# One head group of three V loads on eight of the sixteen DMA engines, 32 KB per read

## The chip, the cores and the metric

The kernel runs on one core of a Trainium2 chip. The metric is the time of one execution on the device in microseconds, read from repeated runs. The experiments ran on several chips, each of them beside runs of the kernel before on the same chip.

## The reference

It is one attention step with a cache: 32 batches, 4 new tokens each, 32 query heads in 4 groups, 2048 cached keys of 128 numbers, all bfloat16.

```python
B, Sq, D = 32, 4, 1024
Hq, Hkv, Sk, Dh = 32, 4, 2048, 128
q = (x @ wq).reshape(B, Sq, Hq, Dh).transpose(0, 2, 1, 3)
scores = einsum("bhqd,bhkd->bhqk", q, repeat(k_cache)) * (Dh ** -0.5)
o = einsum("bhqk,bhkd->bhqd", softmax(scores), repeat(v_cache))
return o.transpose(0, 2, 1, 3).reshape(B, Sq, Hq * Dh) @ wo
```

Keys and values are 2 MB each per batch, 134 MB in all. Nearly all of the kernel's 151 MB of reading is that.

## The kernel before

Each batch is one K load and one V load of 2 MB. K has three buffers in SBUF (the memory on the chip, 128 partitions) and so has V. PE, the matrix engine, transposes K, multiplies with the queries, transposes the probabilities and multiplies with V; ScalarE (ACT in the profile) and VectorE (DVE) move PE's results from PSUM to SBUF and do the softmax. SP issues the loads. The parts that matter here:

```python
def load_k(b):                       # partition = (group, r): 16 KB in one piece per partition
    p.dma("sp", lambda e: e.dma_start(
        K_sb[:, b % NKB, :, :], k_cache[b].rearrange("g (r t) d -> (g r) t d", r=R)),
        [("fill", b - NKB, NFILL - 1)] if b >= NKB else [], ("k", b), f"s_k{b % NKB}")

def load_v(b):                       # 128 partitions x 4 groups x 4 KB
    src = v_cache[b].rearrange("g (p t) d -> p g (t d)", p=128)
    dst = V_sb[:, b % NVB, :, :, :].rearrange("p g t d -> p g (t d)")
    waits = [("pv", b - NVB)] if b >= NVB else []
    if b < B - 1:
        p.dma("sp", lambda e: e.dma_start(dst, src), waits, ("v", b), f"s_v{b % NVB}")
    else:
        ...                          # the last V load: one copy per group

for b in range(NKB):
    load_k(b)
for b in range(B):
    if b + NKB < B:
        load_k(b + NKB)
    load_v(b)
    ...                              # loads 2 to 5 also bring a quarter of wo

def pe_pv(i):
    ...
    waits = waits + [("pt", i, 0), ("pt", i, 1), ("v", i)]
```

In the trace the completion semaphore of a load takes 16 steps. They are read here as one for each of the page's 16 DMA engines that ends its share. The kernel makes PE wait for all 16.

Of the kernel before, what the change touches and what calls it, by code (L numbers as in the profile page):

```python
# [6 lines left out]
ALU = mybir.AluOpType  # L7
AX = mybir.AxisListType
BF16 = mybir.dt.bfloat16
F32 = mybir.dt.float32  # L10


class _Program:
# [43 lines left out]
def bass_standalone__gqa_block_cached__sampling_kernel(  # L57
# [8 lines left out]
    B, Sq, D = x.shape  # L66
# [10 lines left out]
    KT = D // 128  # L77
    NKB = 3
    NVB = 3
    NFILL = 8  # L80
    TB = T // NFILL
    NRING = 4
# [9 lines left out]
    with ExitStack() as es:  # L92
        def sbuf(name, shape, dtype):
            return es.enter_context(nc.sbuf_tensor(name, shape, dtype))
# [3 lines left out]
        K_sb = sbuf("K_sb", [128, NKB, T, Dh], BF16)  # L98
        V_sb = sbuf("V_sb", [128, NVB, G, TV, Dh], BF16)
        KT_sb = sbuf("KT_sb", [128, TV, G, R * C], BF16)  # L100
# [8 lines left out]
        ident = sbuf("ident", [128, 128], BF16)  # L109
        mx = sbuf("mx", [128, B], F32)  # L110
        negmx = sbuf("negmx", [128, B], F32)
        ssum = sbuf("ssum", [128, B], F32)
        rinv = sbuf("rinv", [128, B], F32)

        ps_s = es.enter_context(nc.psum_tensor("ps_s", [128, Sk], F32))
        ps_r = es.enter_context(nc.psum_tensor("ps_r", [128, 4, 512], F32))
        ring = [ps_r[:, i, :] for i in range(NRING)]
# [5 lines left out]
        p = _Program()  # L123
# [8 lines left out]
        def load_k(b):  # L132
# [4 lines that stand above are left out]
        def load_v(b):  # L137
            src = v_cache[b].rearrange("g (p t) d -> p g (t d)", p=128)
            dst = V_sb[:, b % NVB, :, :, :].rearrange("p g t d -> p g (t d)")
            waits = [("pv", b - NVB)] if b >= NVB else []  # L140
            if b < B - 1:
                p.dma("sp", lambda e: e.dma_start(dst, src), waits, ("v", b), f"s_v{b % NVB}")
            else:
                for g in range(G):
                    p.dma("sp", lambda e, g=g: e.dma_start(dst[:, g, :], src[:, g, :]), waits, ("v", b, g), f"s_vl{g}")
# [8 lines left out]
# [4 lines that stand above are left out]
            if b in (2, 3, 4, 5):  # L158
                load_wo(b - 2)
# [21 lines left out]
        for j in (4, 5, 6, 7, 0, 1, 2, 3):  # L181
            src = (ps_s if j < 4 else ps_r[:, :, :].rearrange("p a b -> p (a b)"))[:, (j % 4) * 512:(j % 4 + 1) * 512]
            src = src.rearrange("p (hh b s) -> p hh b s", hh=4, b=B, s=Sq)
            dst = QT_sb[:, :, 4 * j:4 * j + 4, :].rearrange("p b hh s -> p hh b s")
# [9 lines left out]
        def slot(free):  # L194
            n = len(freed)
            freed.append(free)
            return ring[n % NRING], [freed[n - NRING]]
# [3 lines left out]
        def pe_fill(b, f):  # L201
            buf, waits = slot(("kt", b, f))
            buf = slot_of["kt", b, f] = buf.bitcast(BF16)
            for q in range(TB):
                c, v = q // (TB // C), q % (TB // C)
                t = c * TV + f * TB // C + v
                p.op("pe", lambda e, q=q, t=t: e.transpose(  # L207
                    buf[:, q * 128:(q + 1) * 128], K_sb[:, b % NKB, t, :], ident[:, :]),
                    waits + [("k", b), "ident"] if q == 0 else [], ("fill", b, f) if q == TB - 1 else None)
# [25 lines left out]
        def pe_qk(i):  # L235
            waits = [("kt", i, f) for f in range(NFILL)]
            waits += [("qe", j) for j in range(Hq // 4)] if i == 0 else [("exp", i - 1)]
            for c in range(4):
                for g in range(G):
                    p.op("pe", lambda e, c=c, g=g: e.matmul(  # L240
                        ps_s[32 * g:32 * (g + 1), c * 512:(c + 1) * 512],
                        lhsT=QT_sb[:, i, REP * g:REP * (g + 1), :],
                        rhs=KT_sb[:, 4 * c:4 * (c + 1), g, :],
                        start=True, stop=True, tile_position=(0, 32 * g)),
                        waits, ("qk", i) if (c, g) == (3, G - 1) else None)

        def pv_mm(buf, i, g, t, waits, done):
            p.op("pe", lambda e: e.matmul(  # L248
                buf[32 * g:32 * (g + 1), 0:Dh],
                lhsT=PT_sb[:, i % 2, t, 32 * g:32 * (g + 1)],  # L250
                rhs=V_sb[:, i % NVB, g, t, :],
                start=(t == 0), stop=(t == TV - 1), tile_position=(0, 32 * g)), waits, done)

        def pe_pv(i):
            buf, waits = slot(("o", i))
            slot_of["o", i] = buf
            waits = waits + [("pt", i, 0), ("pt", i, 1), ("v", i)]
            for t in range(TV):
                for g in range(G):
                    pv_mm(buf, i, g, t, waits if t == 0 and g == 0 else [],  # L260
                          ("pv", i) if (t, g) == (TV - 1, G - 1) else None)
# [54 lines left out]

        for f in range(NFILL):
            pe_fill(0, f)
            evac(0, f)
        L = B - 1  # L320
        for i in range(B):
            pe_qk(i)
            softmax_max(i)
            if i >= 3:
                pe_ot(i - 3)
                ot_evac(i - 3)
                if i > OG and i % OG == 2:
                    oproj(i // OG - 1)
            if i < L:
                for f in (0, 1):  # L330
                    pe_fill(i + 1, f)
                    evac(i + 1, f)
            softmax_exp(i)
            if i < L:
                for f in range(2, NFILL):
                    pe_fill(i + 1, f)
                    evac(i + 1, f)
            softmax_rinv(i)
            if i >= 2:
                pe_pv(i - 2)  # L340
                o_evac(i - 2)
            if i == L:
                p.op("dve", lambda e: e.tensor_scalar(P_sb[:, :], P_sb[:, :], rinv[:, L:L + 1], None, op0=ALU.mult),  # L343
                     [("rinv", L)], ("pn", L))
            for f in range(2):
                pe_pt(i, f, ("pn", L) if i == L else ("exp", i))
                evac_pt(i, f)


        pe_ot(L - 2)  # L350
        ot_evac(L - 2)
        pe_pv(L - 1)
        o_evac(L - 1)
        y_l = ps_s[:, 0:512]
        n = NOG - 1

        def pv_last(g):
            buf, waits = slot(None)
            for t in range(TV):
                p.op("pe", lambda e, t=t: e.matmul(  # L360
                    buf[:, 0:32], lhsT=V_sb[:, L % NVB, g, t, :], rhs=PT_sb[:, L % 2, t, 32 * g:32 * (g + 1)],
                    start=(t == 0), stop=(t == TV - 1)),
# [77 lines left out]
```

## Time and profile before

| | before |
|---|---|
| time, median | 383.13 us (382.86 to 383.46, 3 runs) |
| DMA load queue, share of 16 engines' span | 97.2% |
| PE, DVE, ACT busy | 72%, 72%, 54% |
| last K load (batch 31) lands | 353.36 us |
| DMA packets, typical time | 4 KB 160 ns, 16 KB 615 ns |

The page cuts the span in 40 slices of 9.5 us. The first line below is the granted PE clock in tenths, the second the busy share of the DMA engines in tenths, the third what they moved in GB/s. Page of the kernel before:

```profile
PEclk9999999999788699999999999999999999999978
DMA  8999999999999999999999999999999999999981
GB/s 328 437 426 420 412 422 410 413 391 411 403 409 412 417 418 420 415 407 417 422 416 413 420 419 412 419 416 417 413 416 420 416 414 420 416 419 410 351 315 32
```

The engines are busy throughout, mostly at 400 to 420 GB/s. The queues on the same page (packets, megabytes, share of the 16 engines' span):

```profile
q1 hardware_dynamic: 27104, 151.49, 97.2%
q8 instruction: 46, 0.75, 0.8%
```

Queue 8 is instruction fetch: 46 packets of 16 KB. The chain of waits that ended last (shares of the span, by engine and then by line) is mostly a wait for K:

```profile
DMA 59%; PE 17%; ACT 11%; DVE 9%; issue 3%; SPq 1%
DMA K_sb<-in_k_cache_dram 52%; DMA V_sb<-in_v_cache_dram 7%; ACT KT_sb L219 6%; ACT P_sb L285 5%; DVE KT_sb L217 5%; PE ps_r L207 4%; PE ps_r L296 3%; DVE mx L280 3%; PE ps_r L248 3%; PE ps_r L225 2%; PE ps_s L240 2%; PE ps_s L296 1%; DVE PT_sb L231 1%; PE ps_r L360 0%; SPq L129 0%
```

In order of time (start, length, what) three pieces of this chain show its end:

```profile
331.59 21.78 DMA K_sb<-in_k_cache_dram
354.07 1.94 ACT KT_sb L219 x2
...
376.33 1.89 PE ps_s L296 x64
```

The last K load lands at 353.4 us (331.59 + 21.78) and about 28 us of compute follow to the end at 381.2. Whatever delays that landing delays the end. The issues of the two big loads (count, KB each, median us from issue to landing):

```profile
K_sb<-in_k_cache_dram SPq DMA_DIRECT2D x32, 2048.0 KB, 25.5
V_sb<-in_v_cache_dram SPq DMA_DIRECT2D x31, 2048.0 KB, 27.2
```

A load lands about 25 us after its issue, five times the 5 us of packets that it is for each engine (32 x 160 ns), so the engines do not run dry for want of issues.

The trace also has the time of each completion step. This list is worked out from it: for a few K loads, when the last of 16 steps came, and how far ahead of it the others were (us, sorted).

```
lands  ahead of the last step
 34.51 [1.91 1.89 1.88 1.86 1.85 1.84 1.81 1.79 | 1.78 1.75 1.66 1.61 1.60 1.33 0.10 0]
127.49 [3.53 3.52 3.46 3.40 3.38 2.81 2.80 2.51 | 1.85 1.76 1.59 1.13 0.34 0.13 0.02 0]
208.90 [5.07 5.03 4.98 4.90 4.86 4.28 4.27 4.01 | 1.48 1.07 0.26 0.22 0.13 0.02 0.01 0]
353.36 [9.65 9.57 9.54 9.47 9.40 8.96 8.29 7.65 | 1.86 1.82 1.77 1.70 1.58 1.57 1.10 0]
```

The engines drift apart in two groups of eight. In the late group one engine after another falls back by about 1.1 us, and each such step comes with an instruction fetch (one fetch packet took 0.95 to 1.35 us). That the fetches cause the drift is read from this order of events, not tested. The 42 fetches before the last landing are 5.6 us for each of eight engines, a little less than the 6.2 to 8.2 us between the early engines and the mean of the late ones; and one early engine too falls back by 1.1 us (between 230 and 240 us). So fetches are most of the drift at best, not all of it. By the last K load eight engines are 7.7 to 9.6 us ahead and wait for nobody, but PE waits for the late eight: its first matmul on these keys starts at 353.41 us, 0.05 us after the last step.

### The profile page before, as it was taken

The page shows a single profiled execution, that of the slowest core. Times are in us where ns is not written, and L with a number is a line of the kernel's source. Part 1 is how long each engine was busy: PE and PEld are TensorE (multiplying, and loading weights), DVE is VectorE, ACT ScalarE, POOL GpSimd, SP SyncE. Part 2 cuts the span into 40 slices and gives each one's busy share as a digit, 9 for nine tenths or more (in the row PEclk, how much of TensorE's full clock was granted, in tenths as well). Part 3 has the DMA queues.
Part 4 walks back from the last instruction along what each step waited for, and adds up shares of the span by engine and source line. Part 5 has one row for each costly group of instructions (what it writes and reads, how often), then busy time and mean ns, then how long its engine had stood idle before and what let it go on. Part 6 is the DMA issues. An engine that isn't in the chain of part 4 may idle for free.

```text
span 381.2 us, 12591 instructions
## 1 busy us (share of the span) xinstructions
PE 275.9 (72%) x5927; PEld 224.2 (59%) x5927; DVE 275.0 (72%) x302; ACT 207.6 (54%) x259; POOL 0.7 (0%) x6
## 2 busy tenths in 40 slices
PE   1876778873837578787777677778776778788756
PEld 1875656662726567666555566666555557566645
DVE  0007999994538395889888885989977876899841
ACT  1006777761615562766666664677655646667630
POOL 0000000000000000000000000000000000000000
PEclk9999999999788699999999999999999999999978
DMA  8999999999999999999999999999999999999981
GB/s 328 437 426 420 412 422 410 413 391 411 403 409 412 417 418 420 415 407 417 422 416 413 420 419 412 419 416 417 413 416 420 416 414 420 416 419 410 351 315 32
DMA packets 27251, 152.32 MB, mean 400 GB/s; under 512 B 1472, under 2 KB 1984, under 8 KB 22592
## 3 DMA queue, kind: packets, MB, share of 16 engines
q1 hardware_dynamic: 27104, 151.49, 97.2%
q8 instruction: 46, 0.75, 0.8%
q10 hardware_dynamic: 96, 0.03, 0.0%
q14 instruction: 5, 0.04, 0.0%
HBM read 151.26 MB, written 0.26 MB: 397 GB/s over the span
## 4 chain that ended last, share of the span: by engine, by line
DMA 59%; PE 17%; ACT 11%; DVE 9%; issue 3%; SPq 1%
DMA K_sb<-in_k_cache_dram 52%; DMA V_sb<-in_v_cache_dram 7%; ACT KT_sb L219 6%; ACT P_sb L285 5%; DVE KT_sb L217 5%; PE ps_r L207 4%; PE ps_r L296 3%; DVE mx L280 3%; PE ps_r L248 3%; PE ps_r L225 2%; PE ps_s L240 2%; PE ps_s L296 1%; DVE PT_sb L231 1%; PE ps_r L360 0%; SPq L129 0%
## 5 line engine op out<-in xcount | busy, mean ns | idle before, releaser
L207 PE MATMUL ps_r<-ident,K_sb 128*128 128x128 bf16 x2048 | 138.5, 225 | 63.3 <-DMA K_sb<-in_k_cache_dram 35.5
L217 DVE COPY KT_sb<-ps_r 128x1024 bf16<-128x1024 bf16 x128 | 148.0, 1216 | 32.8 <-PE ps_r L207 32.6
L207 PEld LDWEIGHTS ps_r<-ident,K_sb 128*128 128x128 bf16 x2048 | 121.2, 101 | 79.7 <-DMA K_sb<-in_k_cache_dram 36.2
L219 ACT ACTIVATE KT_sb<-ps_r 128x1024 bf16<-128x1024 bf16 x128 | 124.3, 1025 | 68.0 <-PE ps_r L207 67.9
L280 DVE TENSOR_REDUCE mx<-ps_s 128x1 f32<-128x2048 f32 x32 | 73.3, 2291 | 8.2 <-PE ps_s L240 5.8
L285 ACT ACTIVATE P_sb<-ps_s,negmx 128x2048 bf16<-128x2048 f32 x32 | 63.0, 1969 | 2.2 <-DVE negmx L281 2.1
L231 DVE COPY PT_sb<-ps_r 128x1024 bf16<-128x1024 bf16 x64 | 41.4, 686 | 16.4 <-PE ps_r L225 15.0
L248 PE MATMUL ps_r<-V_sb,PT_sb 128*32 128x128 bf16 x1984 | 34.2, 223 | 15.3 <-ACT KT_sb L219 8.9
L248 PEld LDWEIGHTS ps_r<-V_sb,PT_sb 128*32 128x32 bf16 x1984 | 28.8, 98 | 20.4 <-ACT KT_sb L219 18.4
L275 ACT ACTIVATE oT_sb<-ps_r 128x128 bf16<-128x128 bf16 x31 | 8.6, 277 | 57.2 <-PE ps_r L271 57.2
L225 PE MATMUL ps_r<-ident,P_sb 128*128 128x128 bf16 x512 | 35.1, 223 | 3.7 <-DVE P_sb L343 3.0
L240 PE MATMUL ps_s<-KT_sb,QT_sb 128*32 128x512 bf16 x512 | 34.3, 382 | 4.5 <-DVE KT_sb L217 1.7
L225 PEld LDWEIGHTS ps_r<-ident,P_sb 128*128 128x128 bf16 x512 | 29.4, 99 | 7.3 <-DVE P_sb L343 3.2
L240 PEld LDWEIGHTS ps_s<-KT_sb,QT_sb 128*32 128x32 bf16 x512 | 10.9, 95 | 15.7 <-issue 4.5
L187 DVE CAST QT_sb<-ps_r 128x512 bf16<-128x512 f32 x2 | 1.3, 687 | 22.6 <-PE ps_r L176 22.6
L265 ACT ACTIVATE o_sb<-ps_r,rinv 128x128 bf16<-128x128 f32 x31 | 11.4, 367 | 10.8 <-PE ps_r L248 10.8
L189 ACT ACTIVATE QT_sb<-ps_r 128x512 bf16<-128x512 f32 x2 | 1.1, 594 | 26.1 <-PE ps_r L176 26.1
L176 PE MATMUL ps_s<-P_sb,w_sb 128*128 128x128 bf16 x128 | 9.3, 230 | 7.8 <-DMA w_sb<-in_wq_dram 7.8
L296 PE MATMUL ps_r<-w_sb,oT_sb 128*32 128x256 bf16 x384 | 11.9, 273 | 3.8 <-issue 2.6
L296 PEld LDWEIGHTS ps_r<-w_sb,oT_sb 128*32 128x32 bf16 x384 | 10.1, 97 | 5.1 <-issue 4.0
L176 PEld LDWEIGHTS ps_s<-P_sb,w_sb 128*128 128x128 bf16 x128 | 8.1, 103 | 8.3 <-issue 4.5
L271 PEld LDWEIGHTS ps_r<-ident,o_sb 128*128 128x128 bf16 x31 | 3.0, 98 | 12.9 <-issue 12.9
(26 smaller groups left out, 62.6 us busy)
## 6 DMA issues: line engine op xcount, KB each, us to landing
K_sb<-in_k_cache_dram SPq DMA_DIRECT2D x32, 2048.0 KB, 25.5
V_sb<-in_v_cache_dram SPq DMA_DIRECT2D x31, 2048.0 KB, 27.2
w_sb<-in_wq_dram SPq DMA_DIRECT2D x4, 2048.0 KB, 14.8
w_sb<-in_wo_dram SPq DMA_DIRECT2D x4, 2048.0 KB, 24.1
V_sb<-in_v_cache_dram SPq DMA_DIRECT2D x4, 512.0 KB, 11.0
P_sb<-in_x_dram SPq DMA_DIRECT2D x1, 256.0 KB, 2.7
out_dram<-y_sb SPq DMA_DIRECT2D x14, 16.0 KB, 8.9
out_dram<-y_sb ACTq DMA_DIRECT2D x2, 16.0 KB, 1.6
```

What stands on the lines that cost most here:

```text
L176: p.op("pe", lambda e, kt=kt, h=h: e.matmul(ps_q(h), lhsT=w_sb[:, kt, h * Dh:(h + 1) * Dh], rhs=xT_sb[:, kt, :], start=(kt == 0 and h % 4 ...
L207: p.op("pe", lambda e, q=q, t=t: e.transpose(buf[:, q * 128:(q + 1) * 128], K_sb[:, b % NKB, t, :], ident[:, :]), waits + [("k", b), "iden ...
L217: p.op("dve", lambda e: e.tensor_copy(dst, src), waits, ("kt", b, f))
L219: p.op("act", lambda e: e.activation(dst, src, ACT.Copy), waits, ("kt", b, f))
L225: p.op("pe", lambda e, q=q: e.transpose(buf[:, q * 128:(q + 1) * 128], P_sb[:, (8 * f + q) * 128:(8 * f + q + 1) * 128], ident[:, :]), wai ...
L231: p.op("dve", lambda e: e.tensor_copy(PT_sb[:, i % 2, 8 * f:8 * f + 8, :].rearrange("p t q -> p (t q)"), buf), [("ptf", i, f)] + ([("pv", ...
L240: p.op("pe", lambda e, c=c, g=g: e.matmul(ps_s[32 * g:32 * (g + 1), c * 512:(c + 1) * 512], lhsT=QT_sb[:, i, REP * g:REP * (g + 1), :], rh ...
L248: p.op("pe", lambda e: e.matmul(buf[32 * g:32 * (g + 1), 0:Dh], lhsT=PT_sb[:, i % 2, t, 32 * g:32 * (g + 1)], rhs=V_sb[:, i % NVB, g, t, : ...
L265: p.op("act", lambda e: e.activation(o_sb[:, :], buf[:, 0:Dh], ACT.Copy, scale=rinv[:, i:i + 1]), [("pv", i), ("rinv", i)] + ([("oT", i - ...
L280: p.op("dve", lambda e: e.tensor_reduce(mx[:, i:i + 1], ps_s[:, :], AX.X, ALU.max), [("qk", i)], ("mx", i))
L285: p.op("act", lambda e: e.activation(P_sb[:, :], ps_s[:, :], ACT.Exp, bias=negmx[:, i:i + 1], scale=scale, accum_out=ssum[:, i:i + 1]), [( ...
L296: p.op("pe", lambda e, h=h, j=j: e.matmul(buf[32 * j:32 * (j + 1), 0:NC], lhsT=oT_sb[:, h, 32 * n:32 * (n + 1)], rhs=wo_sb[:, h, NC * j:NC ...
```

## The change

The intent is to use that lead. In three of the 32 V loads, one group of four (512 KB) leaves the copy over 16 engines and goes in two copies over eight engines. The helper builds a copy whose source is 8 rows of 32 KB and whose destination is 64 partitions of 4 KB, meant for eight engines, each with 8 neighbouring partitions. The trace has no engine numbers.

```diff
@@ -8,6 +8,21 @@
 AX = mybir.AxisListType
 BF16 = mybir.dt.bfloat16
 F32 = mybir.dt.float32
+
+
+def _load_low_half(nc, eng, dst, src):
+
+
+    assert src.shape[0] == 8 and eng.engine == mybir.EngineType.SP
+    return eng.add_instruction(mybir.InstDMACopy(
+        name=nc.get_next_instruction_name(),
+        engine=eng.engine,
+        mode="Copy",
+        queue="qSPDynamicHW",
+        cce_op=ALU.bypass,
+        ins=[eng.lower_ap_dma(src)[0]],
+        outs=[eng.lower_ap_dma(dst)[0]],
+    ))
 
 
 class _Program:
@@ -77,6 +92,7 @@
     KT = D // 128
     NKB = 3
     NVB = 3
+    LOW_V = (7, 15, 23)
     NFILL = 8
     TB = T // NFILL
     NRING = 4
@@ -138,7 +154,13 @@
             src = v_cache[b].rearrange("g (p t) d -> p g (t d)", p=128)
             dst = V_sb[:, b % NVB, :, :, :].rearrange("p g t d -> p g (t d)")
             waits = [("pv", b - NVB)] if b >= NVB else []
-            if b < B - 1:
+            if b in LOW_V:
+                p.dma("sp", lambda e: e.dma_start(dst[:, 0:3, :], src[:, 0:3, :]), waits, ("v", b, 0), f"s_v{b % NVB}")
+                low = v_cache[b, 3].rearrange("(j a t) d -> j a (t d)", j=2, a=8)
+                for j in range(2):
+                    p.dma("sp", lambda e, j=j: _load_low_half(nc, e, dst[64 * j:64 * (j + 1), 3, :], low[j]),
+                          waits, ("v", b, 1) if j == 0 else ("v", b), "s_vlow")
+            elif b < B - 1:
                 p.dma("sp", lambda e: e.dma_start(dst, src), waits, ("v", b), f"s_v{b % NVB}")
             else:
                 for g in range(G):
@@ -254,7 +276,7 @@
         def pe_pv(i):
             buf, waits = slot(("o", i))
             slot_of["o", i] = buf
-            waits = waits + [("pt", i, 0), ("pt", i, 1), ("v", i)]
+            waits = waits + [("pt", i, 0), ("pt", i, 1), ("v", i)] + ([("v", i, 0)] if i in LOW_V else [])
             for t in range(TV):
                 for g in range(G):
                     pv_mm(buf, i, g, t, waits if t == 0 and g == 0 else [],
```

## The prediction

> **What bounds it now.** The DMA engines. The page shows them 97.2% busy on the load queue; the chain of waits is 59% DMA (K loads 52%), while PE and DVE are each 72% busy. By packet, the trace has 16 KB taking 615 ns, 4 KB 160 ns and 2 KB 88 ns, so one 2 MB K or V load takes the 16 engines about 4.9 to 5.1 us.
>
> The sixteen completion increments of each load are not together. Early (K load at 29 us) fifteen lie within 0.6 us; at 127 us eight engines are 2.5 to 3.5 us ahead of the last, at 209 us 4.0 to 5.1, at 348 us 7.7 to 9.6, and the other eight within 1.9. The only extra load is queue 8, instruction fetch: 46 packets of 16 KB, each 1.03 to 1.35 us. They visit the eight late engines in turn (each step of the late group is about 1.1 us). So a load counts as landed up to 9.6 us after half of its engines are done. I take the late eight to be the upper ones; the trace has no engine numbers.
>
> **What the change does.** Three times (loads 7, 15, 23), 512 KB of V leaves the 16-engine copy. The upper eight lose 8 packets of 4 KB each time, 24 x 160 ns = 3.84 us in all; the lower eight gain as much (32 KB more each; 32 KB reads save only some 8 ns per packet, an estimate from 160 and 615 ns). The lead of 9.6 us shrinks by 7.7 us to about 2. Compute instructions are unchanged; SP issues two more copies per such load, off the path, since loads wait about 25 us in the queue.
>
> **On the critical path.** The last K load lands at 353.4 us, and 28 us of compute follow it to the end. All three moves precede it, so if the upper engines save their 3.84 us, everything shifts: 379.3 us.
>
> **Why I expect less.** [...] Engines run at 25.6 to 26.6 GB/s here (4096/160, 16384/615)[...].
>
> So two outcomes: about 379.3 without port contention, 383 to 389 with it.
>
> **Prediction: 384 us, range 378.8 to 390.** Faster by over 2%: 0.01; within 2%: 0.88; slower by over 2%: 0.11.
>
> **What would show it.** Rebalancing right: at the last K load the spread of the increments falls from 9.6 to about 2 us and it lands about 3.8 us earlier. Port contention: packets of the small copies, and those of upper engines beside them, well over 160 ns per 4 KB (320 or more); the last K load lands at 353 us or later; the order of early and late halves flips. PE, DVE and ACT busy times should stay within 1%.
>
> **What would make it wrong.** The late eight being the lower ones (then 3.8 us slower or worse); lower engines' skew avoiding port collisions; a start-up cost of the 8-engine copies.

The sum came to this: 383.1 us less 3.84 us is 379.3 us; with a loss from writes that get in each other's way, 383 to 389 us; the forecast is 384 us. The terms that lead from 379.3 to 383 to 389 us rested on rules of the hardware that no trace or run here shows.

## More of the kernel before

Busy time by stretch, with PE clock, DMA share and GB/s as the last three columns:

```profile
core 0: us, PE busy (x) PEld busy (x) DVE busy (x) ACT busy (x) POOL busy (x), PEclk, DMA share, GB/s
120.00:135.00 15.00, 8.75 (x163) 7.42 (x161) 8.42 (x9) 6.36 (x8) 0.00 (x0) 0.77 1.01 415
135.00:150.00 15.00, 11.48 (x275) 8.85 (x276) 12.15 (x13) 6.63 (x9) 0.00 (x0) 1.00 1.02 419
218.00:233.00 15.00, 10.94 (x288) 9.10 (x289) 10.54 (x11) 6.45 (x9) 0.00 (x0) 1.00 1.02 419
303.00:318.00 15.00, 11.96 (x303) 9.78 (x300) 9.53 (x12) 7.47 (x10) 0.00 (x0) 1.00 1.02 416
```

## The result, and the profile after

| | before | after |
|---|---|---|
| time, median | 383.16 us (4 runs) | 396.12 us (395.22 to 397.65, 4 runs) |
| ratio of fast runs | | 1.0342, 95% interval 1.0308 to 1.0377 |
| last K load lands | 353.36 us | 366.16 us |
| PE, DVE, ACT busy us | 275.9, 275.0, 207.6 | 282.7, 275.0, 207.6 |

Ratios here are the mean time of one kernel's fast runs over that of the other's of the same rounds, so they are not quite the ratios of the medians.

The kernel became 13 us slower, outside the predicted range. The same lines of the page after:

```profile
PEclk9989999997968888999999969999999899999989
DMA  8999999999999999999999999999999999999970
GB/s 332 430 426 428 416 418 401 410 394 412 411 395 413 428 286 415 416 416 419 417 417 411 360 334 416 417 413 418 417 417 417 326 350 418 405 420 397 365 263 24
```

The rate is as before in most slices. It drops in three places, one for each load that was split: 286 GB/s in slice 15, then 360 and 334, then 326 and 350. The engines count as busy there, so they are not waiting for issues. Queues of the kernel after:

```profile
q1 hardware_dynamic: 26816, 151.49, 97.0%
q8 instruction: 46, 0.75, 0.8%
```

Bytes and instruction fetches are unchanged. The chain of waits of the kernel after:

```profile
DMA 54%; PE 20%; ACT 11%; DVE 9%; issue 2%; SPq 2%
DMA K_sb<-in_k_cache_dram 35%; DMA V_sb<-in_v_cache_dram 14%; ACT KT_sb L241 6%; DMA w_sb<-in_wq_dram 6%; DVE KT_sb L239 5%; PE ps_r L229 5%; ACT P_sb L307 5%; PE ps_r L270 4%; DVE mx L302 4%; PE ps_r L247 3%; PE ps_r L318 3%; PE ps_s L262 3%; SPq L17 1%; PE ps_s L318 1%; PE ps_s L198 1%
```

and its end in order of time:

```profile
343.97 22.19 DMA K_sb<-in_k_cache_dram
366.86 1.94 ACT KT_sb L241 x2
...
388.55 1.89 PE ps_s L318 x64
```

The last K load lands at 366.16 us (343.97 + 22.19), 12.8 us later than before, and the compute behind it has kept its length. So the loss is made before that landing, in the DMA. The issues after, with the queue as deep as before:

```profile
K_sb<-in_k_cache_dram SPq DMA_DIRECT2D x32, 2048.0 KB, 26.3
V_sb<-in_v_cache_dram SPq DMA_DIRECT2D x28, 2048.0 KB, 26.8
```

Busy time by stretch of the kernel after, with the same columns as before:

```profile
120.00:135.00 15.00, 8.36 (x159) 7.03 (x157) 8.19 (x9) 6.36 (x8) 0.00 (x0) 0.77 1.02 419
135.00:150.00 15.00, 9.61 (x175) 7.79 (x176) 9.21 (x11) 6.36 (x8) 0.00 (x0) 0.82 1.01 329
218.00:233.00 15.00, 7.31 (x161) 5.84 (x161) 9.02 (x11) 7.09 (x9) 0.00 (x0) 0.90 1.01 324
303.00:318.00 15.00, 9.66 (x174) 7.99 (x171) 10.54 (x12) 9.29 (x12) 0.00 (x0) 0.89 1.02 329
```

The stretch from 120 to 135 us is as before. The three that hold an event fall from 416 to 419 GB/s to 324 to 329, with the DMA share still at 1.01 or more.

What slowed is in the packets. This table is worked out from the packet records of the kernel after around the first event: for packets that start in each half microsecond, the count and the median ns (range).

```
 us     4 KB packets          16 KB packets         32 KB packets
136.0   37  162 (159-172)     4   615 (615-615)
137.0   46  161 (159-172)                           2  1652 (1553-1751)
138.0   26  185 (175-441)     1   939               1  2136
138.5   14  274 (260-351)     1  1102               2  2456
139.0   12  321 (287-339)     1  1155               2  2608
141.0    9  294 (289-304)     2  1164 (1155-1173)   1  2272
143.0                         6  1034 (1027-1049)
145.5    4  162 (159-166)    10   613 (611-622)
```

In the kernel before, every half microsecond from 136 to 142 us has medians of 159 to 167 and 614 to 619 ns. After, packets of every kind take 1.5 to 2.3 times as long for some 6 us (from 138.5 to 144.5 us), with no group that is spared. The 48 packets of 32 KB took 2.04 us on average, against 1.22 at the pace of 16 KB packets (an estimate: 615 ns, plus the time per byte between 4 and 16 KB).

Summed over all load packets, the time above the usual 160, 615, 88 and (estimated) 1222 ns grew by 11.1 us per engine. The last K load's completion steps show the rest:

```
after  366.16 [14.07 14.03 | 8.53 8.48 8.39 8.33 8.32 7.97 7.95 7.78 7.15 6.80 6.64 5.21 | 0.08 0]
```

There are no longer eight and eight, but two far ahead, twelve together and two that are 5.2 us behind everybody. The sum closes: the sixteen steps come 10.6 us later on average than before, and the last one is 7.5 us behind the average in place of 5.2. Together that is the 12.8 us by which the load lands later: some 10.6 us for slow packets and 2.2 us for the two stragglers.

### The profile page after: what moved, and what is told of

Read it like the earlier page. It is cut to its first block, busy times and chain, and to the rows that moved or that the text cites. A ratio compares the mean times of both kernels' runs of the same rounds, so it can differ in the third digit from the quotient of the medians.

```text
span 393.4 us, 12597 instructions
## 1 busy us (share of the span) xinstructions
PE 282.7 (72%) x5927; PEld 231.2 (59%) x5927; DVE 275.0 (70%) x302; ACT 207.6 (53%) x259; POOL 0.7 (0%) x6
## 3 DMA queue, kind: packets, MB, share of 16 engines
q1 hardware_dynamic: 26816, 151.49, 97.0%
## 4 chain that ended last, share of the span: by engine, by line
DMA 54%; PE 20%; ACT 11%; DVE 9%; issue 2%; SPq 2%
DMA K_sb<-in_k_cache_dram 35%; DMA V_sb<-in_v_cache_dram 14%; ACT KT_sb L241 6%; DMA w_sb<-in_wq_dram 6%; DVE KT_sb L239 5%; PE ps_r L229 5%; ACT P_sb L307 5%; PE ps_r L270 4%; DVE mx L302 4%; PE ps_r L247 3%; PE ps_r L318 3%; PE ps_s L262 3%; SPq L17 1%; PE ps_s L318 1%; PE ps_s L198 1%
## 5 line engine op out<-in xcount | busy, mean ns | idle before, releaser
L229 PE MATMUL ps_r<-ident,K_sb 128*128 128x128 bf16 x2048 | 140.1, 226 | 62.4 <-DMA K_sb<-in_k_cache_dram 36.5
L229 PEld LDWEIGHTS ps_r<-ident,K_sb 128*128 128x128 bf16 x2048 | 122.5, 102 | 79.1 <-DMA K_sb<-in_k_cache_dram 38.5
L270 PE MATMUL ps_r<-V_sb,PT_sb 128*32 128x128 bf16 x1984 | 35.5, 227 | 25.7 <-DMA V_sb<-in_v_cache_dram 12.3
L270 PEld LDWEIGHTS ps_r<-V_sb,PT_sb 128*32 128x32 bf16 x1984 | 30.0, 101 | 30.8 <-ACT KT_sb L241 15.8
L247 PE MATMUL ps_r<-ident,P_sb 128*128 128x128 bf16 x512 | 36.4, 228 | 3.3 <-DVE P_sb L365 3.1
L247 PEld LDWEIGHTS ps_r<-ident,P_sb 128*128 128x128 bf16 x512 | 30.8, 102 | 7.1 <-DVE P_sb L365 3.3
L198 PE MATMUL ps_s<-P_sb,w_sb 128*128 128x128 bf16 x128 | 11.0, 254 | 6.2 <-DMA w_sb<-in_wq_dram 6.2
L198 PEld LDWEIGHTS ps_s<-P_sb,w_sb 128*128 128x128 bf16 x128 | 9.8, 116 | 6.6 <-issue 4.5
L318 PEld LDWEIGHTS ps_r<-w_sb,oT_sb 128*32 128x32 bf16 x384 | 10.2, 97 | 3.1 <-issue 2.0
```

Source lines behind the costliest of these rows:

```text
L198: p.op("pe", lambda e, kt=kt, h=h: e.matmul(ps_q(h), lhsT=w_sb[:, kt, h * Dh:(h + 1) * Dh], rhs=xT_sb[:, kt, :], start=(kt == 0 and h % 4 ...
L229: p.op("pe", lambda e, q=q, t=t: e.transpose(buf[:, q * 128:(q + 1) * 128], K_sb[:, b % NKB, t, :], ident[:, :]), waits + [("k", b), "iden ...
L247: p.op("pe", lambda e, q=q: e.transpose(buf[:, q * 128:(q + 1) * 128], P_sb[:, (8 * f + q) * 128:(8 * f + q + 1) * 128], ident[:, :]), wai ...
L270: p.op("pe", lambda e: e.matmul(buf[32 * g:32 * (g + 1), 0:Dh], lhsT=PT_sb[:, i % 2, t, 32 * g:32 * (g + 1)], rhs=V_sb[:, i % NVB, g, t, : ...
L318: p.op("pe", lambda e, h=h, j=j: e.matmul(buf[32 * j:32 * (j + 1), 0:NC], lhsT=oT_sb[:, h, 32 * n:32 * (n + 1)], rhs=wo_sb[:, h, NC * j:NC ...
```

## The experiments

Two theories stood at first. *Port theory* (that of the prediction): two engines that write certain partitions at the same time slow each other, and nobody else. *Wide-read theory*: a 32 KB read that feeds eight rows of 4 KB is slow by itself and slows the other engines. Later a third came in, *fabric theory*: such meetings slow all engines. The expectations also call it *stall-all*, and the port theory *local port theory*. Two engines that write such partitions together are called a pair here.

By the author's account, two forms did not build: a copy with a source of three dimensions (8 x 8 x 4 KB), and a scratch buffer for additional loads, for which SBUF had no room.

Each row of a small copy's source is counted as one engine. In six runs, the load queue has just the packets that this gives, with one packet of 4 bytes per row (foreign_dose: the 27104 of the kernel before, less 1152 of 4 KB, plus 84 of 16 KB and 84 of 4 bytes, is 26120). For the other runs it is taken to hold.

### 4 KB reads in place of 32 KB

```diff
-for j in range(2):
-    ... _load_low_half(nc, e, dst[64 * j:64 * (j + 1), 3, :], low[j]) ...
+for q in range(16):                 # 8 partitions, 8 apart, one for each of eight engines
+    h = 64 * (q // 8) + q % 8
+    ... e.dma_start(dst[h:h + 57:8, 3, :], src[h:h + 57:8, 3, :]) ...
```

> The same bytes to the same partitions from the same eight engines, but by sixteen copies of 8 partitions with 4 KB reads in place of two with 32 KB reads. Port theory (only the shared SBUF ports slow packets, the read size is nothing): as slow as the change, 391 to 397 us, low engines' 4 KB packets 300 ns or more. Wide-read theory (a 32 KB read that feeds eight 4 KB rows slows itself and every other engine, whatever port): the loss goes and the rebalancing shows, 379 to 382 us, 4 KB packets near 160 ns.

Measured: correct, 397.87 us, ratio 1.0377 (1.0345 to 1.0409). Around the first event the medians per half microsecond reach 311 ns for 4 KB packets and 1196 ns for 16 KB packets. The width of the reads and the helper are not the cause: plain copies that fill the same partitions with 4 KB reads lose as much (0.9 us above the 391 to 397 us that the port theory gave).

### Four neighbouring partitions per engine

```diff
-low = ... (j a t) d -> j a (t d)", j=2, a=8        # 64 partitions a copy
+low = ... (j a t) d -> j a (t d)", j=4, a=8        # 32 partitions a copy, 16 KB reads
```

With this edit each of the eight engines writes four neighbouring partitions per copy. The first two copies fill partitions 0 to 63, the last two 64 to 127.

> Four copies of 32 partitions with 16 KB reads per load: each of the eight engines writes four neighbouring partitions[...]. Port theory: packets of the first two copies near 615 ns, of the last two near 1230; 382 to 385 us in all. Wide-read theory: a 16 KB read that feeds four rows still slows every engine for the whole event, 386 to 393 us, and 4 KB packets beside the first two copies rise to 250 ns or more.

Measured: correct, 393.24 us, ratio 1.0259 (1.0244 to 1.0275). The trace separates the copies by the engines that come first. While these are in the first two (137 to 138.4 us) the medians are 160 to 164 and 627 to 638 ns. When they reach the last two (the first completion steps of the small copies come at 138.6 us), the medians rise to 313 and 1227 ns (139.5 us), with no packet spared, and stay high until 144 us. Both kinds read the same way, and only the destination differs. So the cause is where the data is written; the run of the first two copies alone, below, confirms it. But the port theory's size is wrong: it allowed 382 to 385 us and no slow packets beside those of the last two copies. The time is near the 386 to 393 us of the wide-read theory, but that one wanted slow packets beside the first two copies.

### All sixteen engines, 8 neighbouring partitions on each

```diff
-low = ... "(j a t) d -> j a (t d)", j=2, a=8
-for j in range(2): ...
+low = v_cache[b, 3].rearrange("(a t) d -> a (t d)", a=16)
+... _load_low_half(nc, e, dst[:, 3, :], low) ...    # one copy, 16 rows of 32 KB
```

> The group of 512 KB in one wide copy over all 16 engines, 32 KB reads, 8 neighbouring partitions on each; nothing is moved between halves. Port theory: [...]32 KB packets near 2.4 us in place of 1.22, others undisturbed: about 1.2 us lost per event, 386 to 388 us. Wide-read theory: 32 KB packets slow and packets of other engines beside them at 250 ns or more, 388 to 396 us.

Measured: correct, 391.87 us, ratio 1.0226 (1.0211 to 1.0241). Nothing is moved between engines here: 16 engines have one packet of 32 KB each in place of 8 of 4 KB (the load queue's 26816 packets fit this), and the last K load has no stragglers (a gap of 1.1 us, in the table at the end). Since the width of the reads is no cause (reads_4k), the loss of 8.7 us is from the places that each engine writes. The port theory's 386 to 388 us is missed. The time lies in the range of the wide-read theory, which the 4 KB reads had ruled out already. Busy time by stretch of this kernel (columns as before):

```profile
120.00:135.00 15.00, 8.45 (x160) 7.14 (x158) 8.17 (x9) 6.36 (x8) 0.00 (x0) 0.77 1.02 419
135.00:150.00 15.00, 9.60 (x173) 7.67 (x174) 9.30 (x11) 6.36 (x8) 0.00 (x0) 0.81 1.01 327
218.00:233.00 15.00, 9.85 (x232) 8.18 (x233) 9.21 (x11) 7.66 (x11) 0.00 (x0) 0.89 1.01 344
303.00:318.00 15.00, 10.35 (x240) 8.86 (x241) 9.55 (x12) 7.83 (x11) 0.00 (x0) 0.89 1.02 335
```

### Only partitions 0 to 63, wrong result

```diff
-for j in range(2):
-    ... dst[64 * j:64 * (j + 1), 3, :], low[j] ...
+... dst[0:64, 3, :], low[0] ...                     # the upper half of the group is not loaded
```

> Wrong result on purpose: only the first of the two low copies (partitions 0 to 63); partitions 64 to 127 of that group keep old data. Port theory: [...]their packets stay at 160 and 615 ns while the low engines' 32 KB packets take about 2.4 us; the upper engines gain their 3.84 us: 378 to 381 us. Wide-read theory: the upper engines' packets rise to 250 ns or more beside the 32 KB packets, and half of the loss stays: 384 to 390 us.

Measured: 387.77 us, ratio 1.0126 (1.0105 to 1.0147). The small copies here are on eight engines alone and fill partitions 0 to 63 alone. Still the 4 KB packets beside the 32 KB packets reach a median of 309 ns, none of that half microsecond under 241, and a kernel that loads 0.79 MB less is slower. The rate over the 40 slices dips at all three events:

```profile
GB/s 328 432 432 412 421 414 412 408 395 413 408 403 412 417 342 413 421 412 410 420 415 419 390 378 413 416 419 415 420 414 419 366 390 417 414 414 409 363 302 18
```

Both theories of that moment fail: the wide read was out already, and the port theory wanted the packets of the upper engines ("their packets" in the expectation) to stay at 160 and 615 ns.

### The same half, four neighbouring partitions per engine, wrong result

```diff
 # as the four aligned copies, but only the first two
-for j in range(4):
+for j in range(2):
```

> Wrong result on purpose: only the first two of the four aligned copies (partitions 0 to 63, four neighbouring partitions on each of the eight low engines); partitions 64 to 127 of that group keep old data. So [...]the low engines move the same bytes as in the kernel before, the upper engines 24 packets of 4 KB less each. If the eight late engines are the upper ones and port sharing was the whole cost: 379.3 us (378.5 to 380.2), all packets at 160 and 615 ns, the last K load 3.8 us earlier than before. If the late engines are the lower ones: 383 us. If the raw copies on eight engines cost something of their own: 381 us or more, slow packets beside them.

Measured: 381.42 us, ratio 0.9955 (0.9943 to 0.9968, 5 rounds). The slow packets are gone (medians 159 to 167 and 611 to 638 ns through the events), and the stretches show it:

```profile
120.00:135.00 15.00, 8.84 (x165) 7.51 (x162) 8.41 (x9) 6.36 (x8) 0.00 (x0) 0.77 1.02 420
135.00:150.00 15.00, 11.54 (x275) 8.90 (x276) 12.17 (x14) 6.64 (x9) 0.00 (x0) 1.00 1.01 415
218.00:233.00 15.00, 11.20 (x289) 9.14 (x290) 10.32 (x11) 6.36 (x8) 0.00 (x0) 1.00 1.02 418
303.00:318.00 15.00, 13.29 (x309) 11.27 (x307) 9.56 (x11) 7.75 (x10) 0.00 (x0) 0.92 1.01 413
```

So the copies on eight engines slow no packet by themselves. But the gain is 1.6 us, not 3.8, which none of the three readings had foreseen (the third allowed this time, but with slow packets). The completion steps say why. The first row is the V load of batch 15 without its last group, the second the K load behind it:

```
222.53 [5.82 5.04 4.77 4.75 4.29 3.94 3.66 3.59 | 1.30 1.28 1.17 1.15 1.07 0.96 0.11 0]
228.71 [7.04 6.28 4.73 4.72 4.29 3.93 3.68 3.58 | 2.53 2.52 2.41 2.40 2.31 2.21 0.08 0]
```

An engine that is not in the copy is relieved of 8 packets of 4 KB and gains 1.28 us on one that is. Eight gain about 1.2 us: two of the early group and six of the late one. Eight do not: six early ones and the last two. So the eight engines of the copy are not the eight early engines. Two of them are late ones, which got no relief, and PE waits for those two.

### Two engines alone: four, and two neighbouring partitions on each, wrong results on purpose

```diff
 # two_own: two copies, 4 neighbouring partitions on each engine
+for m in range(2):
+    ... dst[32 * m:32 * m + 8, 3, :] <- 2 rows of 16 KB ...
 # two_shared: the same 16 partitions, four copies, 2 partitions on each engine
+for h in (0, 4, 32, 36):
+    ... dst[h:h + 4, 3, :] <- 2 rows of 8 KB ...
```

> Wrong result on purpose, control of the next run: per event two copies on engines 0 and 1 alone, partitions 0 to 7 and 32 to 39, four neighbouring partitions on each engine[...]; the rest of the group is not loaded. Both theories: 379 to 380 us (the upper engines save 3.84 us), 160 and 615 ns packets throughout.

> Wrong result on purpose: the same bytes, engines and partitions as in the control, in four copies of four partitions[...]. Local port theory (only the engines on the shared port slow): two engines at 600 ns per 8 KB in place of some 310, the other fourteen at 160 and 615 ns; 379 to 380 us as the control. Stall-all theory (a port with two writers halves the pace of all sixteen engines while it lasts): 4 KB packets of all engines at 250 to 330 ns and 16 KB packets near 1000 to 1230 for some 2.5 to 5 us per event; 382 to 387 us.

Measured: 379.28 us, ratio 0.9907 (0.9892 to 0.9923), and 379.27 us, ratio 0.9902 (0.9887 to 0.9917). Both agree with the 379.3 that the prediction worked out for 3.84 us less work on the late engines. In the second, the 8 KB packets took 309 to 574 ns, not the 600 of a lasting meeting, so the two engines seem to have been apart in time for much of it. The 4 KB packets of all engines kept medians of 159 to 177 ns. The stall-all expectation missed; the run is weak evidence because of the short overlap.

### Two plain copies of 64 partitions, meant for all sixteen engines

```diff
+for j in range(2):
+    ... e.dma_start(dst[64 * j:64 * (j + 1), 3, :], src[64 * j:64 * (j + 1), 3, :]) ...
```

> Group 3 in two plain copies of 64 partitions (0 to 63, 64 to 127) over all sixteen engines, 4 KB reads, correct result: no raw copies, no work moved between engines[...]. Local port theory: [...]about 0.6 us lost per copy at most: 383.5 to 386 us. Stall-all theory: all packets near twice their time for 3 to 5 us per event: 387 to 392 us. If sixteen engines on plain copies do not collide: 383 us.

Measured: correct, 393.29 us, ratio 1.0263 (1.0249 to 1.0277): 10.2 us lost by cutting three groups in halves, with plain copies and no work meant to be moved (the last K load has a gap of 1.1 us, against 5.2 in the change). The rate over the 40 slices shows the same three dips as the change:

```profile
GB/s 335 434 429 410 410 411 409 412 391 415 407 400 411 418 291 409 417 421 411 416 420 412 354 358 417 417 417 418 415 416 416 313 355 415 416 418 411 363 314 47
```

What cost the time is that everything in flight slowed (10.7 us per engine of slow packets for 10.2 us lost). The 387 to 392 us of the stall-all expectation were nearly met, the 383.5 to 386 of the local one were not.

### How many pairs it takes: two engines, four, eight

```diff
+k = {7: 2, 15: 4, 23: 8}[b]         # k engines, 12 packets of 8 KB on each, partitions 0 to 63
+todo = [(g, h) for s in (0, 2 * k) for g in (1, 2, 3) for h in (s, 32 + s)]
+... dst[h:h + 2 * k, g, :] <- k rows of 8 KB ...   # 2 partitions on each engine
```

> Wrong result on purpose, read by packets and landings, not by time. Groups 1 to 3 of loads 7, 15 and 23 are not loaded but for copies of two neighbouring partitions per engine, all to partitions 0 to 63: engines 0 and 1 at load 7, 0 to 3 at load 15, 0 to 7 at load 23, each 96 KB in 12 packets of 8 KB[...]. Stall-all by any shared port: 4 KB packets of the other engines at 250 to 330 ns in all three events. Stall-all that needs many shared ports: the other engines near 160 ns with one pair, between with two, 250 or more with four; 8 KB packets about 620 ns in all three. Landings: engines that get no such copy gain 3.84 us per event on those that do. If the eight late engines (those of the instruction fetch) are all outside engines 0 to 7, all late ones gain in every event; if two of them are inside, as the landings of even_aligned and of the change suggest (12 engines together, two 5 us behind, two 5 us ahead), at load 23 only six late ones gain and two stay behind.

Measured (single look, 395.23 us, not comparable in time because most of three V loads is missing). The rate by slice:

```profile
GB/s 338 430 426 420 420 416 400 410 397 411 408 397 413 420 407 414 419 413 420 414 420 367 396 412 388 416 418 415 417 341 252 287 397 375 340 415 380 252 250 17
```

At load 7 there is no dip. From 136 to 142 us the two engines' 8 KB packets take 601 to 641 ns but for three of them, twice the 311 of an undisturbed one, and the others stay at medians of 159 to 176 and 611 to 652 ns. One pair slows itself alone. At load 15 the engines came in one after another. While two 8 KB packets took 950 to 990 ns each, one 16 KB packet took 1929 ns, about three times the usual 311 and 615: three engines in each other's way, it seems, and the others rose to about 200 and 760 ns, a quarter. At load 23 the others reach some 330 and 1200 to 1260 ns, twice the usual, in about half of the event (23 of 42 half microseconds from 291 to 312 us have a 4 KB median of 300 ns or more), and less between. The landings that the expectation asks for were not evaluated.

### Partitions 64 and up, four neighbouring ones per engine: two engines, four, eight

```diff
+k = {7: 2, 15: 4, 23: 8}[b]
+todo = [(g, h) for g in (1, 2, 3) for h in (64, 96)]
+... dst[h:h + 4 * k, g, :] <- k rows of 16 KB ...  # 4 neighbouring partitions on each engine
```

> Wrong result on purpose, read by packets. Groups 1 to 3 of loads 7, 15, 23 are loaded only by six copies of 16 KB per engine to partitions 64 and up, four neighbouring partitions on each engine, [...]two such ports at load 7, four at load 15, eight at load 23. Local port theory: moving engines' and those owners' 16 KB packets near 1230 ns, all others at 615 and 160, at every dose. Fabric theory (enough shared ports slow everything): others near 160 ns at two ports, between at four, 300 or more at eight, as in aligned_16k.

The "owner" is the engine that a moving engine was meant to meet. Who it is was assumed.

Measured (single look, 398.47 us, not comparable in time). The rate by slice:

```profile
GB/s 339 425 430 430 415 413 400 407 404 409 410 397 417 366 324 416 414 419 419 415 417 372 218 374 416 414 418 415 416 415 253 225 354 417 402 414 402 339 265 12
```

At load 7, with two moving engines, the first 1.5 us (134.5 to 136) show medians of 159 to 185 and 683 to 759 ns, and then, from 136.5 to 142 us, 311 to 332 and 1197 to 1278 ns for everybody. Four and eight moving engines give the same factor, some 320 to 340 and 1200 to 1270 ns on their plateaus. So there is no smooth dose. Two moving engines already halve the pace of all the rest, and more do not make it worse, only longer. The end of the last event shows one moving engine. The steps of the small copies come in pairs until 319.7 us (318.40 and 318.46, 319.69 and 319.74), and from 317 to 318.5 us the medians are still 340 and 1275 ns. After that one moving engine is left, with steps some 1.2 us apart, the last at 323.47. From 320 to 322.5 us two interleaved rows of 16 KB packets take 1225 to 1260 ns, while no 4 KB packet takes over 180 ns and all but one of the other 16 KB packets take 612 to 658 ns. So a single pair slows only itself, here as in the run before, and two moving engines, read as two pairs, slow everybody. That the first stretch at load 7 was also a time with one active pair is a reading of the order of events, not shown.

### Four engines, four neighbouring partitions on each, wrong result

```diff
 # as two_own, with 4 engines: partitions 0 to 15 and 32 to 47
+... dst[32 * m:32 * m + 16, 3, :] <- 4 rows of 16 KB ...
```

> Wrong result on purpose: as even_aligned, but on engines 0 to 3 alone (partitions 0 to 15 and 32 to 47 of group 3[...]; the rest of the group is not loaded). If two of the eight late engines are among engines 4 to 7, every late engine is now relieved of 3.84 us: 379.3 us as with engines 0 and 1 alone, and the two stragglers of even_aligned are gone. If the late two are among 0 to 3: 381 us or more, as even_aligned. If even_aligned lost its 2 us to something else about copies on few engines: between the two.

Measured: 379.46 us, ratio 0.9907 (0.989 to 0.9925), with no dip:

```profile
GB/s 328 425 433 423 411 416 417 410 397 411 398 414 415 413 418 418 416 413 417 414 415 418 419 418 414 419 414 417 418 413 419 419 415 414 415 415 413 379 314 20
```

The last three steps of the final K load come 1.32, 1.20 and 0 us before its end, with no pair of stragglers. With four engines in the copies in place of eight, all late engines gain. So none of these four seems to be late. The two late ones of even_aligned may be among the other four of the copies there, but that needs these four to be among those eight, which is not shown.

### One event in place of three

```diff
-LOW_V = (7, 15, 23)
+LOW_V = (15,)
```

> The change at load 15 alone. If the loss is made event by event: a third of 13 us, 387.5 us (386.5 to 388.5). If it needs the build-up of engine skew over three events: less than 386.5.

Measured: correct, 387.05 us, ratio 1.0108 (1.0091 to 1.0125). It is a third of the loss, 4.2 of 13 us, as the expectation said for a loss that is made event by event.

### Together

"Slow packets" is the time above the usual per packet, summed and divided by 16 engines, less that of the kernel before. "Gap" is by how much the last completion step of the last K load trails the third from last.

| kernel | time us | slow packets, us | last K load lands | gap us |
|---|---|---|---|---|
| before | 383.1 | 0 | 353.4 | 1.6 |
| the change | 396.1 | 11.1 | 366.2 | 5.2 |
| reads_4k | 397.9 | 11.7 | 367.5 | 5.1 |
| aligned_16k | 393.2 | 8.8 | 363.9 | 5.5 |
| even_only (wrong result) | 387.8 | 5.6 | 357.6 | 3.5 |
| wide_all16 | 391.9 | 9.4 | 362.3 | 1.1 |
| halves_16 | 393.3 | 10.7 | 363.7 | 1.1 |
| one_event | 387.1 | 4.3 | 357.4 | 1.0 |
| even_aligned (wrong result) | 381.4 | 0.3 | 351.7 | 2.0 |
| two_own, two_shared, four_own (wrong results) | 379.3 to 379.5 | 0 to 0.3 | 349.3 to 349.6 | 0.9 to 1.3 |

## Why the prediction was wrong

- **What bounds the kernel: right.** The time followed the landing of the last K load in every run (12.8 us later in the change, 13 us slower).
- **3.84 us for eight packets less, three times: right.** The runs with two and four engines alone gave 379.3 and 379.5 us, against 379.3 worked out.
- **Writes in each other's way as the danger: right in kind.** With four neighbouring partitions per engine in partitions 0 to 63 no median rose (159 to 167 ns for 4 KB in even_aligned); with eight, 32 KB packets took 1.3 to 2.7 us in the change.
- **The step that failed first** put the loss on the engines that meet, mostly hidden in their lead of 9.6 us. The runs showed in its place that all sixteen engines fall to about half their pace (foreign_dose with two moving engines: 311 to 332 ns for 4 KB and 1197 to 1278 for 16 KB, for everybody). In the change, 20 us of half-microsecond slices have a median packet over 1.4 times the usual; half a pace for that long is about 10 us, near the 11.1 us summed from packets. The late engines lose it as well, so no lead hides it. That a meeting is only a local matter holds for a single pair (the first event of pairs_dose, 601 to 641 ns per 8 KB for these two; the end of foreign_dose, 1225 to 1260 per 16 KB).
- **The step that failed second:** "I take the late eight to be the upper ones". Two of the late eight were among the eight that took the copies (even_aligned: six late steps gained 1.2 us, two did not). They had their instruction fetches and 3 x 32 KB more, while the other late ones were relieved. That is the gap of 5.2 us in the change. It is absent (1.1 us) in wide_all16 and halves_16, where all packets slow down but no work is moved.
- **"The order of early and late halves flips": wrong.** Two engines went far ahead and two far behind. PE's busy time rose 2.5%, not 1% at most, at a granted clock of 0.944 against 0.963; DVE and ACT did not move.
- **The outcome "about 379.3 without port contention" was not to be had,** even apart from slow packets: the two late engines inside the copies would have had 3.84 us more work, which makes about 387 us (an estimate: 383.1 + 3.84). The prediction had named this case, late engines among the lower ones, under what would make it wrong.

What stays open: why two pairs, and not one, halve every engine, and which partitions make a pair. No run tried a cause for either. Which two engines are late is not known; they were among the eight of the copies in even_aligned. No version that beats both kernels came out: every correct run, whether it moved work or not, was slower than the kernel before (387.1 to 397.9 us). A version that has only one pair active at a time, the case that slowed two engines alone, was not tried.

## What to carry to other kernels

Before you split a load, measure what its pieces do to the packets of all other traffic. Here the plain loads of 128 partitions ran at 160 and 615 ns per packet; halves of 64 partitions cost 10.2 us and eight neighbouring partitions per engine 8.7 us, and all traffic in flight slowed, not only the copy that was changed. Four neighbouring partitions per engine slowed nothing in partitions 0 to 63 (even_aligned) and everything in 64 to 127 (aligned_16k, 313 and 1227 ns). Before you rebalance engines, find out which ones are late by a small copy on few engines and the shift of the completion steps; equal counts are not equal sets.
